# One array tile per head for the products with the states, another order of steps in each window, and x loaded first

## The chip, the cores and the metric

The kernel runs on one core of a Trainium2 chip. Its engines work side by side, each through its own list of instructions in order: TensorE (PE; its weight loads are shown as PEld), VectorE (DVE), ScalarE (ACT), GpSimd (POOL) and SyncE (SP), which here issues most transfers between HBM and the on-chip memory SBUF. TensorE writes into PSUM, eight banks of 128 x 512 float32. The metric is the device time of the whole program in microseconds (us).

## The reference

Three parts in a row, in float32 on the chip, with factors cut into a high and a low part where accuracy wants it:

```python
scores = scale * x @ state.T          # per head: 512 x 32
xread  = softmax(scores) @ state      # every x reads the 32 states
scores2 = scale * state @ x.T
sread  = softmax(scores2) @ x         # every state reads all x
t = concat([xread, sread])            # 4 batches x (512+32) tokens, 8 heads x 64 = 512 columns
h = t @ w_in;  g = where(h >= 1, h, where(h <= -1, 0, (h + 1)**2 / 4));  t = g @ w_out
h = t @ w_in2; g = max(h, 0) + log1p(exp(-abs(h)));                      t = g @ w_out2
```

The weights are 512 x 2048 and 2048 x 512 and arrive as 64-bit floats; 2,176 tokens go through.

## The kernel before, in words

The read of the states is not carried out for x: since `xread = a @ state`, the first layer for a batch is `a @ (state @ w_in)`, and the kernel makes G = state @ w_in for each batch, 256 columns of w_in (a *pair* of 128-column blocks, 8 pairs) at a time. These are the products with the states (`g_mm`, L404). A head has 64 of the 512 columns and 32 states, so one head's product is 64 rows deep and 32 columns wide on the array. Before, two heads share one product: `stb` holds both heads' states on the diagonal of a 128 x 64 block, with zeros beside them, and four products of 128 x 64 with 256 columns fill one PSUM bank. The scores (`scores`, L213) use the same blocks.

G is then cut in two by `g_split`: ScalarE copies it rounded (`gh`, L67), VectorE subtracts for the residue (`gl`, L70). Products of full accuracy are made of three, high x high, high x low and low x high; `ahi` and `alo` are the two parts of the softmax of the scores.

The main loop runs over 148 *windows*. A window is one 128-wide block of the hidden layer for one tile of tokens: 16 for each of batches 0, 1 and 2, 4 for the states that were read ("s"), 16 for batch 3, then five tiles of 16 for the second network. One pass of the loop works for three windows at once: `l1(w)` makes the first layer of the newest (six products, L501), `close(v)` ends the activation of the one before it on VectorE (L584), `l2(u)` adds the second layer of the window three back into four accumulators (L441 to L443). All engines take their instructions in the order in which the loop writes them. A pass of the loop gives: l1, then the products with the states on TensorE, then a first step of the attention of a coming batch (`hops`, one step per `yield`), `close`, `l2`, the split of second-layer weights (L67 `wh`, GpSimd `wl`), `act_open` (L573, L574), the rebuild of coming weights, `cut_hi`, `cut_lo`, then `g_split`, then the scaling of the next weights, then a second step of hops, and last the issue of a transfer.

Weights arrive as 64-bit numbers, a pair (1 MB) at a time, in one of two `ws` buffers. ScalarE scales the upper words in place (L107), VectorE shifts and ors the halves together (`rebuild`, L123 and L124; into `w1_p` for w_in, which traces show as `w`, and into `cv` for w_out). The plan is a list of due windows: `plan_pair(Pair(w1, True, p, W1), 2 * (p - 1))` and `plan_pair(Pair(w2, ...), 2 * p + 1)`; a pair is scaled in the pass before its due pass, and the transfer into a buffer is issued at the due pass of the pair two before it. The first w_in pair comes in `wh`, the second in `wl`, before the loop.

PSUM: two rotating banks "at" serve the products with the states, the scores, the transposes of x (L198) and of scores (`s_turn`) and the read by the states (L265); two "l1", four accumulators.

Of the kernel before, what the change touches and what calls it, by code (L numbers as in the profile page):

```python
# [18 lines left out]
def fused_kernel(ctx: ExitStack, tc: tile.TileContext, x, state, w1, w2, w3, w4, out):  # L19
# [43 lines left out]
    def bank(tag, bufs):  # L63
        return new(psum, [P, 512], F32, tag, bufs)

    def copy(dst, src):
# [80 lines left out]
    make_identity(nc, ident)  # L147
    stb = new(p1, [P, NJ, B, 2 * N], F32, "stb")
    nc.gpsimd.memset(stb, 0.0)
    x1s = new(p1, [P, NJ, B * N], F32, "x1s")  # L150
# [24 lines left out]
    def place_state(st):  # L175
        ps = bank("at", 2).rearrange("p (j c) -> p j c", j=NJ)
        for j in range(NJ):
            nc.tensor.transpose(ps[:, j, :], st[:, 2 * j : 2 * j + 2, :].rearrange("p e d -> p (e d)"), ident)
        for e in range(2):
            sl = slice(e * D, (e + 1) * D)  # L180
            nc.vector.tensor_copy(
                stb[sl, :, :, e * N : (e + 1) * N], ps[sl].rearrange("p j (b n) -> p j b n", n=N)
            )

# [4 lines left out]
    class Attn:  # L189
# [18 lines left out]

        def scores(self, g):
            self.ps[g] = bank("at", 2)  # L210
            for i in range(2):
                j = 2 * g + i
                nc.tensor.matmul(  # L213
                    self.ps[g][64 * i : 64 * i + 64, :], stb[:, j, self.b, :], self.xT[j], start=True, stop=True
                )

# [25 lines left out]
        def s_turn(self, g):  # L242
            self.ps[g] = bank("at", 2)
# [12 lines left out]

        def s_read(self, js):
            xb = xt[self.b]
            if 0 in js:
                self.ps["s"] = bank("at", 2)  # L260
            for j in js:
                for r in range(R):
                    for e in range(2):
                        c0 = (2 * (j % 2) + e) * N
                        nc.tensor.matmul(  # L265
                            self.ps["s"][e * D : (e + 1) * D, j * N : (j + 1) * N],
                            xb[:, r, 2 * j + e, :],
                            self.a2T[j // 2][:, r, c0 : c0 + N],
                            start=(r == 0),
                            stop=(r == R - 1),  # L270
                        )
# [35 lines left out]
        def hops(self):  # L307

            for js in ((0, 1), (2,), (3,)):
                ps = [bank("at", 2) for _ in js]  # L310
# [7 lines left out]
            self.scores(0)  # L318
            yield
            self.s_copy(0)  # L320
            yield
            self.scores(1)
            yield
            self.s_copy(1)
            self.blocks(0)
# [26 lines left out]
            yield  # L352
            self.s_read((0, 1))
            yield
            self.n_hi(0)
            if self.b < 3:
                self.n_lo(0)
            self.n_back(1)
            yield
            self.s_read((2, 3))  # L360
# [5 lines left out]
            self.s_out()  # L366
            yield
# [5 lines left out]
        def rest(self):  # L373
            yield
            for g in range(NG):
                self.s_max(g)
            yield
            yield
            for g in range(NG):
                self.s_exp(g)  # L380
            yield
            yield
            for g in range(NG):
                self.s_norm(g)
# [6 lines left out]
            self.s_read((0, 1, 2, 3))  # L391
            yield
            self.s_out()
            yield
# [11 lines left out]
    def g_split(b, p, ps):  # L406
        hi = new(p1, [P, NG * C2], F32R, "gh", 2)
        lo = new(p1, [P, NG * C2], F32R, "gl", 2)
        copy(hi, ps)
        sub(nc.vector, lo, ps, f32(hi))  # L410
        G[b, p] = [t.rearrange("p (g f) -> p g f", g=NG) for t in (hi, lo)]

# [118 lines left out]
    def evac(w):  # L531
        if w.ph == 1 and w.tl == "s":
# [3 lines left out]
            def pe():  # L536
                ps = bank("at", 2)
                for k in range(NK):
# [95 lines left out]
    def plan_g(i, b, p):  # L634
        def pe():
            ps = bank("at", 2)
            g_mm(b, p, ps)
            return lambda: g_split(b, p, ps)
# [39 lines left out]
    with tc.manual_schedule():  # L678
        nc.scalar.preload_act_table_set("natural_log_exp_and_others")
        st = load_state()  # L680
        early = [pair for a, pair in pairs[:4]]
# [7 lines left out]
        warm(8)  # L689
        first.scale()  # L690
        first.conv()
        ps = bank("l1", 2)
        g_mm(0, 0, ps)
        g_split(0, 0, ps)
        a0 = Attn(0)
# [4 lines left out]
        for j in range(NJ):  # L700
            a0.x_copy(j, ps[j], j % 2 == 0)
        for g in range(NG):
            a0.scores(g)
        for g in range(NG):
            a0.blocks(g, a0.ps[g])
            a0.n_sub(g, (nc.vector, nc.gpsimd)[g])
        for g in range(NG):
            a0.s_copy(g)
            a0.n_exp(g)
        early[0].scale()  # L710
# [74 lines left out]
```

## Time and profile before

| what | value |
|---|---|
| median of 3 runs | 771.84 us (771.06 to 772.34) |
| profiled execution, whole time | 772.06 us |
| its span, first to last instruction | 770.2 us |
| busy: PE, PEld | 743.0 (96%), 606.3 (79%) |
| busy: DVE, ACT, POOL | 437.3 (57%), 458.3 (60%), 103.7 (13%) |
| granted clock of TensorE, mean | 0.99 |
| HBM read, written | 42.47 MB, 8.91 MB |

Busy time is the time that an engine spent in instructions, whether or not anybody waited for them. Shares over the whole span mix stages: GpSimd's 13% are 6 or 7 tenths of the time near the start and nothing in the second half. Beside busy times the trace gives for each instruction what ended the wait before it, and from these the chain of work that ended last.

### The profile page before, as it was taken

The page shows a single profiled execution, that of the slowest core. Times are in us where ns is not written, and L with a number is a line of the kernel's source. Part 1 is how long each engine was busy: PE and PEld are TensorE (multiplying, and loading weights), DVE is VectorE, ACT ScalarE, POOL GpSimd, SP SyncE. Part 2 cuts the span into 40 slices and gives each one's busy share as a digit, 9 for nine tenths or more (in the row PEclk, how much of TensorE's full clock was granted, in tenths as well). Part 3 has the DMA queues.
Part 4 walks back from the last instruction along what each step waited for, and adds up shares of the span by engine and source line. Part 5 has one row for each costly group of instructions (what it writes and reads, how often), then busy time and mean ns, then how long its engine had stood idle before and what let it go on. Part 6 is the DMA issues. An engine that isn't in the chain of part 4 may idle for free.

```text
span 770.2 us, 9775 instructions
## 1 busy us (share of the span) xinstructions
PE 743.0 (96%) x3768; PEld 606.3 (79%) x3768; DVE 437.3 (57%) x695; ACT 458.3 (60%) x800; POOL 103.7 (13%) x60
## 2 busy tenths in 40 slices
PE   5599899999999999999999999999999999999997
PEld 4366677867767788777888888888889998998986
DVE  4877964245337424555599984554654554555543
ACT  3677675445545435566778775655655666566563
POOL 0265670002000001122222320000000000000000
PEclk9799999999999999999999999999999999999999
DMA  9466363300010003144343400300020002001001
GB/s 289 110 217 217 109 194 81 55 1 1 1 55 1 1 1 110 56 128 159 110 164 110 164 0 1 96 1 1 0 89 9 1 0 83 1 1 41 1 1 41
DMA packets 39582, 52.00 MB, mean 68 GB/s; under 512 B 19312, under 2 KB 21872, under 8 KB 39536
## 3 DMA queue, kind: packets, MB, share of 16 engines
q1 hardware_dynamic: 36912, 50.73, 21.1%
q10 hardware_dynamic: 2624, 0.66, 0.4%
q8 instruction: 29, 0.48, 0.3%
q14 instruction: 17, 0.14, 0.1%
HBM read 42.47 MB, written 8.91 MB: 67 GB/s over the span
## 4 chain that ended last, share of the span: by engine, by line
PE 92%; DVE 4%; ACT 2%; DMA 1%; POOL 1%; issue 0%; SPq 0%; DVEq 0%; ACTq 0%
PE acc L441 16%; PE acc L442 16%; PE acc L443 16%; PE l L501 10%; PE l L443 8%; PE l L441 8%; PE l L442 8%; PE at L404 4%; PE l L488 2%; PE at L265 1%; PE at L213 1%; DMA wh<-in_moe_w_in_dram 1%; DVE w L124 1%; PE at L198 1%; DVE w L123 1%; POOL wl L70 0%
## 5 line engine op out<-in xcount | busy, mean ns | idle before, releaser
L70 DVE TENSOR_TENSOR gtl<-tl,gth 128x384 fp32r<-128x384 f32 (+1 forms) x80 | 48.9, 611 | 148.6 <-ACT gth L67 148.6
L577 ACT ACTIVATE ta<-l 128x384 f32<-128x384 f32 (+1 forms) x80 | 42.8, 535 | 128.7 <-PE l L443 128.7
L573 ACT ACTIVATE ta<-l 128x512 f32<-128x512 f32 x68 | 40.6, 598 | 128.2 <-PE l L501 104.3
L70 DVE TENSOR_TENSOR gtl<-ta,gth 128x512 fp32r<-128x512 f32 x52 | 36.0, 692 | 136.6 <-ACT gth L67 136.6
L442 PE MATMUL acc<-wl,gth 128*128 128x512 f32 x288 | 113.3, 393 | 0.0
L441 PE MATMUL acc<-wh,gth 128*128 128x512 f32 x288 | 113.2, 393 | 0.0
L443 PE MATMUL acc<-wh,gtl 128*128 128x512 f32 x288 | 112.7, 391 | 0.0
L441 PE MATMUL acc<-gth,wh 128*128 128x512 f32 x256 | 104.7, 409 | 0.0
L443 PE MATMUL acc<-gth,wl 128*128 128x512 f32 x256 | 100.2, 391 | 0.4 <-POOL wl L70 0.4
L442 PE MATMUL acc<-gtl,wh 128*128 128x512 f32 x256 | 100.3, 392 | 0.0
L70 POOL TENSOR_TENSOR wl<-cv,wh 128x1024 fp32r<-128x1024 f32 x24 | 62.8, 2615 | 220.8 <-ACT wh L67 219.5
L443 PE MATMUL l<-x,wl 128*128 128x384 f32 (+1 forms) x192 | 68.7, 358 | 0.0
L441 PE MATMUL l<-x,wh 128*128 128x384 f32 (+1 forms) x192 | 68.6, 357 | 0.0
L442 PE MATMUL l<-x,wh 128*128 128x384 f32 (+1 forms) x192 | 68.5, 357 | 0.0
L443 PEld LDWEIGHTS acc<-wh,gtl 128*128 128x128 f32 x288 | 54.1, 188 | 12.2
L441 PEld LDWEIGHTS acc<-gth,wh 128*128 128x128 f32 x256 | 48.1, 188 | 19.1 <-issue 9.1
L441 PEld LDWEIGHTS acc<-wh,gth 128*128 128x128 f32 x288 | 54.1, 188 | 11.2 <-issue 0.8
L442 PEld LDWEIGHTS acc<-wl,gth 128*128 128x128 f32 x288 | 54.0, 188 | 10.0
L443 PEld LDWEIGHTS acc<-gth,wl 128*128 128x128 f32 x256 | 48.1, 188 | 11.6 <-POOL wl L70 0.8
L70 DVE TENSOR_TENSOR tl<-tl,ta 128x384 f32<-128x384 f32 (+1 forms) x80 | 55.3, 691 | 2.8
L588 DVE SCALAR_TENSOR_TENSOR ta<-tb,ta 128x384 f32<-128x384 f32 (+1 forms) x80 | 55.9, 698 | 0.0
L442 PEld LDWEIGHTS acc<-gtl,wh 128*128 128x128 f32 x256 | 48.2, 188 | 8.8
(114 smaller groups left out, 1376.2 us busy)
## 6 DMA issues: line engine op xcount, KB each, us to landing
ws<-in_moe_w_out_dram SPq DMA_DIRECT2D x16, 1024.0 KB, 4.8
ws<-in_moe_w_in_dram SPq DMA_DIRECT2D x14, 1024.0 KB, 5.5
xd<-xs SPq DMA_DIRECT2D x16, 256.0 KB, 2.9
out_dram<-xs SPq DMA_DIRECT2D x16, 256.0 KB, 2.5
x<-in_x_dram SPq DMA_DIRECT2D x14, 256.0 KB, 6.2
xs<-xd SPq DMA_DIRECT2D x8, 256.0 KB, 6.3
wh<-in_moe_w_in_dram SPq DMA_DIRECT2D x2, 512.0 KB, 5.5
wl<-in_moe_w_in_dram SPq DMA_DIRECT2D x2, 512.0 KB, 7.7
```

The source lines that it names most:

```text
L70: eng.tensor_tensor(dst, a, b, op=ALU.subtract)
L123: nc.vector.tensor_scalar(d, lo, 29, None, op0=ALU.logical_shift_right)
L124: nc.vector.scalar_tensor_tensor(d, hi, 3, d, op0=ALU.logical_shift_left, op1=ALU.bitwise_or)
L404: nc.tensor.matmul(o, stb[:, j, b, :], W1[p][:, j, :], start=True, stop=True)
L441: nc.tensor.matmul(o, lh, rh, start=first, stop=False)
L442: nc.tensor.matmul(o, lh, rl, start=False, stop=False)
L443: nc.tensor.matmul(o, ll, rh, start=False, stop=last)
L488: nc.tensor.matmul(w.h[:, i * P : (i + 1) * P], W1[f // 2][:, k, (f % 2) * P : (f % 2 + 1) * P], x1s[:, k, :], start=(k == 0), stop=(k == ...
L501: nc.tensor.matmul(w.h, l[:, g, f], r[:, g, :], start=i == 0, stop=i == len(terms) - 1)
L573: nc.scalar.activation(w.a, w.hc, AF.Relu, bias=1.0)
L577: nc.scalar.activation(w.a, w.hc, AF.Abs)
L588: nc.vector.scalar_tensor_tensor(w.a, w.b, 1.0, w.a, op0=ALU.subtract, op1=ALU.subtract)
```

## The change

Four things. The states lie in `stT` without zeros, and `heads` makes one product per head, 64 rows by 32 columns, on eight places of the array: the row half e, and the 32-column block j. The heads of the upper rows write one PSUM bank and those of the lower rows another. The rotating banks "at" become one tile `side` of two banks; steps that need one bank take its halves in turn (`at_bank`), products with the states and scores take both. The loop's pass puts the products with the states and `g_split` behind the scaling and the second step of hops. At the start, x is loaded ahead of all weights, its scores come before the first weights are rebuilt, and two multiplications and both residues go to GpSimd.

```diff
+    side = new(psum, [P, 2, 512], F32, "at")
+    def at_bank():
+        turn[0] ^= 1
+        return side[:, turn[0] ^ 1, :]
...
+    def heads(b, o, rhs):
+        for j in range(NJ):
+            for e in range(2):
+                rows = slice(e * D, (e + 1) * D)
+                nc.tensor.matmul(
+                    o(e)[j * N : (j + 1) * N, :], stT[rows, j, b * N : (b + 1) * N], rhs(j)[rows], start=True, stop=True
+                )
...
-    def g_mm(b, p, ps):
-        for j in range(NJ):
-            i = j % 2
-            o = ps.rearrange("p (g f) -> p g f", g=NG)[64 * i : 64 * i + 64, j // 2, :]
-            nc.tensor.matmul(o, stb[:, j, b, :], W1[p][:, j, :], start=True, stop=True)
+    def g_mm(b, p, two=None):
+        o = (lambda e: side[:, e, :C2]) if two is None else (lambda e: two[e][:, :C2])
+        heads(b, o, lambda j: W1[p][:, j, :])
...
-        plan_pair(Pair(w1, True, p, W1), 2 * (p - 1))
+        plan_pair(Pair(w1, True, p, W1), max(2 * p - 3, -1))
     for p in range(NP):
-        plan_pair(Pair(w2, False, p, W2, lambda: pools["b"]), 2 * p + 1)
+        plan_pair(Pair(w2, False, p, W2, lambda: pools["b"]), 2 * p)
...
-                plan_g(t0 + 2 * p - (1 if b == 0 else 2), b, p)
+                plan_g(t0 + 2 * p - 2, b, p)
...
         first = Pair(w1, True, 0, W1)
         first.load("wh", nc.sync)
-        load_x(0, [nc.scalar, nc.sync])
...
-            a0.n_norm(g, nc.vector)
+            a0.n_norm(g, (nc.vector, nc.gpsimd)[g])
+        for g in range(NG):
+            sub(nc.vector, lo[:, g, :], two[g][:, :C2], f32(hi[:, g, :]))
         for g in range(NG):
             a0.n_back(g)
             a0.n_hi(g)
-            a0.n_lo(g, nc.vector)
+            a0.n_lo(g, nc.gpsimd)
+        run(-1, "conv")
+        run(-1, "late")
...
-            rests = [f() for f in post] + run(i, "pe")
+            for f in post:
+                f()()
...
-            for f in rests:
-                f()
             run(i, "late")
             for g in list(gens.values()):
                 next(g, None)
+            run(i, "pe")
             run(i, "load")
```

(`load_x` now stands ahead of `first`.) In `hops` the two steps of scores become one, as do the two of the read by the states, and steps without work keep their places. In the changed kernel the small products have line 194, l1 508, l2 448 to 450, copies 75, residues 78, scaling 115, the rebuild 131 and 132, `close` 591 and `act_open` 580 and 581.

TensorE, the first three windows of the loop, before (`l1_46`, `l1_49` and `l1_58` are their first layers, `gh_21` and `gh_55` the first and second pair of G):

```order
L501 MATMUL l1_46_216<-ahi_23_139,gh_21_135 128x512 x2
L501 MATMUL l1_46_216<-alo_24_140,gh_21_135 128x512 x2
L501 MATMUL l1_46_216<-ahi_23_139,gl_22_136 128x512 x2
L501 MATMUL l1_49_232<-ahi_23_139,gh_21_135 128x512 x2
L501 MATMUL l1_49_232<-alo_24_140,gh_21_135 128x512 x2
L501 MATMUL l1_49_232<-ahi_23_139,gl_22_136 128x512 x2
L404 MATMUL at_50_239<-w1_1_48_226,stb_2_74 64x256 x4
L501 MATMUL l1_58_262<-ahi_23_139,gh_55_255 128x512 x2
L501 MATMUL l1_58_262<-alo_24_140,gh_55_255 128x512 x2
L501 MATMUL l1_58_262<-ahi_23_139,gl_56_256 128x512 x2
```

and now (`l1_46`, `l1_52` and `l1_60`):

```order
L508 MATMUL l1_46_229<-ahi_19_121,gh_32_176 128x512 x2
L508 MATMUL l1_46_229<-alo_20_122,gh_32_176 128x512 x2
L508 MATMUL l1_46_229<-ahi_19_121,gl_33_177 128x512 x2
L194 MATMUL at_1_69<-w1_1_44_218,stT_3_75 32x256 x8
L508 MATMUL l1_52_257<-ahi_19_121,gh_32_176 128x512 x2
L508 MATMUL l1_52_257<-alo_20_122,gh_32_176 128x512 x2
L508 MATMUL l1_52_257<-ahi_19_121,gl_33_177 128x512 x2
L508 MATMUL l1_60_282<-ahi_19_121,gh_49_251 128x512 x2
L508 MATMUL l1_60_282<-alo_20_122,gh_49_251 128x512 x2
L508 MATMUL l1_60_282<-ahi_19_121,gl_50_252 128x512 x2
```

The group for the second pair moved ahead of the first layer of window 1, and is eight small products in place of four.

ScalarE, window 3 before, up to the next window's first step (`gh_76` is a pair of G, `ws_65` weights that have just landed, `wh_84` a half of second-layer weights):

```order
L573 ACTIVATE ta_72_316<-l1_66_287 128x512
L574 ACTIVATE ta_72_316<-ta_72_316 128x512
L67 ACTIVATE gth_74_322<-ta_61_274 128x512
L67 ACTIVATE gh_76_326<-at_67_294 128x512
L107 ACTIVATE ws_65_285<-ws_65_285 128x1024
L67 ACTIVATE wh_84_365<-cv_73_319 128x1024
L573 ACTIVATE ta_86_369<-l1_81_335 128x512
```

and window 4 now, in which a copy of G stands again (`at_1` is the tile of two banks, `xT` the turned x of the next batch):

```order
L580 ACTIVATE ta_83_386<-l1_82_358 128x512
L581 ACTIVATE ta_83_386<-ta_83_386 128x512
L75 ACTIVATE gth_85_392<-ta_75_343 128x512
L115 ACTIVATE ws_79_354<-ws_79_354 128x1024
L75 ACTIVATE xT0_87_397<-at_1_69 128x512
L75 ACTIVATE xT1_88_399<-at_1_69 128x512
L75 ACTIVATE gh_89_409<-at_1_69 128x512
L75 ACTIVATE wh_93_439<-cv_84_389 128x1024
```

The scaling of `ws` and two copies of x now stand ahead of `gh`, which stood ahead of them.

VectorE at the end of the start, before (`alo_24` are the residues of the softmax, `ta_47` the activation of window 0, `w1_1` the second w_in pair, `cv_52` the first w_out pair):

```order
L298 STREAM_TRANSPOSE sa_44_207<-sa_37_180 128x512
L70 TENSOR_TENSOR alo_24_140<-sa_44_207,ahi_23_139 128x512
L123 TENSOR_SCALAR w1_1_48_226<-wl_13_99 128x512
L124 SCALAR_TENSOR_TENSOR w1_1_48_226<-wl_13_99,w1_1_48_226 128x512
L123 TENSOR_SCALAR w1_1_48_226<-wl_14_100 128x512
L124 SCALAR_TENSOR_TENSOR w1_1_48_226<-wl_14_100,w1_1_48_226 128x512
L584 SCALAR_TENSOR_TENSOR ta_47_223<-ta_47_223,l1_46_216 128x512
L123 TENSOR_SCALAR cv_52_248<-ws_15_103 128x1024
L124 SCALAR_TENSOR_TENSOR cv_52_248<-ws_15_103,cv_52_248 128x1024
L70 TENSOR_TENSOR gl_56_256<-at_50_239,gh_55_255 128x512
```

and now (`w1_1_44`, `cv_48` and `ta_47_236` are the same three):

```order
L307 STREAM_TRANSPOSE sa_43_214<-sa_36_183 128x512
L131 TENSOR_SCALAR w1_1_44_218<-wl_14_99 128x512
L132 SCALAR_TENSOR_TENSOR w1_1_44_218<-wl_14_99,w1_1_44_218 128x512
L131 TENSOR_SCALAR w1_1_44_218<-wl_15_100 128x512
L132 SCALAR_TENSOR_TENSOR w1_1_44_218<-wl_15_100,w1_1_44_218 128x512
L131 TENSOR_SCALAR cv_48_239<-ws_16_103 128x1024
L132 SCALAR_TENSOR_TENSOR cv_48_239<-ws_16_103,cv_48_239 128x1024
L78 TENSOR_TENSOR gl_50_252<-at_1_69,gh_49_251 128x512
L591 SCALAR_TENSOR_TENSOR ta_47_236<-ta_47_236,l1_46_229 128x512
```

The residue `alo` has left VectorE, and the first rebuild into `cv` and `gl` now stand ahead of the close of window 0.

## Rows read from the trace of the kernel before

**Rows 1.** Busy time by stage: the stretch (us), its length, busy us of each engine with its instructions in brackets, TensorE's granted clock, the share of time that the DMA engines were busy, GB/s. The cuts are the first step of window 0 on ScalarE (29.36), of window 16 (112.56), of window 68 (376.30), and the end.

```profile
0.00:29.36 29.36, 14.12 (x59) 10.25 (x60) 17.20 (x30) 9.13 (x14) 2.64 (x8) 0.79 0.84 223
29.36:112.56 83.20, 76.29 (x414) 55.91 (x415) 67.07 (x79) 61.15 (x94) 51.96 (x29) 0.99 0.52 174
112.56:376.30 263.74, 263.74 (x1475) 204.85 (x1474) 124.46 (x207) 140.62 (x245) 26.73 (x16) 1.00 0.19 55
376.30:770.20 393.90, 388.85 (x1824) 335.28 (x1822) 228.61 (x380) 247.41 (x448) 22.38 (x9) 1.00 0.13 42
```

**Rows 2.** The chain of work that ended last, over the whole span, as shares: by engine, and by engine, tile and line.

```profile
PE 92%; DVE 4%; ACT 2%; DMA 1%; POOL 1%; issue 0%; SPq 0%; DVEq 0%; ACTq 0%
PE acc L441 16%; PE acc L442 16%; PE acc L443 16%; PE l L501 10%; PE l L443 8%; PE l L441 8%; PE l L442 8%; PE at L404 4%; PE l L488 2%; PE at L265 1%; PE at L213 1%; DMA wh<-in_moe_w_in_dram 1%; DVE w L124 1%; PE at L198 1%; DVE w L123 1%; POOL wl L70 0%
```

**Rows 3.** The same chain in order of time, at small products and behind them: start (us), us, engine, tile, line, instructions.

```profile
60.40 1.01 PE at L404 x8
61.42 0.86 PE at L213 x4
62.28 0.43 PE acc L441
62.70 0.23 PE acc L442
...
65.22 1.40 PE l L501 x6
66.62 1.01 PE at L213 x4
...
103.07 0.90 PE at L265 x32
...
284.14 3.57 PE l L488 x32
```

**Rows 4.** TensorE's wait for the state over the span (us, how often, the longest), and the chain in the start, as in rows 3.

```profile
PE at L178 <- DMA xT<-in_state_dram: 3.9, 1, 3.9
...
15.98 0.73 DVE sa L224
24.80 0.69 DVE alo L70
```

**Rows 5.** Busy time in three stretches of the start, columns as in rows 1: with the weights under way, with x under way behind them, and with TensorE mostly idle.

```profile
12.00:18.00 6.00, 4.44 (x21) 2.96 (x20) 3.77 (x6) 1.68 (x3) 0.00 (x0) 0.86 1.04 397
19.50:23.50 4.00, 0.00 (x0) 0.00 (x0) 3.79 (x9) 1.73 (x3) 1.05 (x1) 0.63 1.32 220
20.51:30.75 10.24, 4.72 (x10) 3.39 (x11) 7.57 (x16) 4.34 (x8) 0.11 (x1) 0.50 0.41 67
```

**Rows 6.** The timeline of single instructions around one weight pair in the loading stage, by engine (ScalarE, VectorE, GpSimd, SyncE): start (us), us, engine, line, operation, out<-in, shapes, in square brackets the idle time before it and what ended it; and from the page the issues of w_in transfers: how many, KB each, us from issue to landing.

```profile
52.24 0.58 ACT L67 ACTIVATE gh<-at 128x512 fp32r<-128x512 f32 x1
52.72 1.14 ACT L107 ACTIVATE ws<-ws 128x1024 f32<-128x1024 f32 x1
54.23 1.05 ACT L67 ACTIVATE wh<-cv 128x1024 fp32r<-128x1024 f32 x1
44.54 0.68 DVE L123 TENSOR_SCALAR w<-ws 128x1024 uint32<-128x1024 uint32 x1
45.33 1.23 DVE L124 SCALAR_TENSOR_TENSOR w<-ws,w 128x1024 uint32<-128x1024 uint32 x1
47.27 2.10 DVE L123 TENSOR_SCALAR cv<-ws 128x1024 uint32<-128x1024 uint32 x1
49.48 2.12 DVE L124 SCALAR_TENSOR_TENSOR cv<-ws,cv 128x1024 uint32<-128x1024 uint32 x1
52.85 0.69 DVE L70 TENSOR_TENSOR gl<-at,gh 128x512 fp32r<-128x512 f32 x1 [1.25 <-ACT gh L67]
45.50 3.33 POOL L70 TENSOR_TENSOR wl<-cv,wh 128x1024 fp32r<-128x1024 f32 x1 [1.31 <-PE at L198]
46.59 0.37 SPq L95 DMA_DIRECT2D ws<-in_moe_w_in_dram  x1
ws<-in_moe_w_in_dram SPq DMA_DIRECT2D x14, 1024.0 KB, 5.5
```

**Rows 7.** From the loading stage, 26 to 116 us (the last row from 90 to 112): waits (the waiting instruction, what ended the wait, sum in us, count, the longest in us); the rebuilds of w_in, of w_out's residues and of others by tile (count, then shortest/median/longest ns, and the stretch); residues alo on GpSimd (count, busy us, mean ns, idle before).

```profile
ACT ws L107 <- DMA ws<-in_moe_w_in_dram: 2.5, 1, 2.5
PEld l L501 <- ACT gh L67: 3.8, 2, 1.9
PE at L404 <- DVE s L238: 1.4, 1, 1.4
L123 DVE TENSOR_SCALAR w<-ws x6: 684/686/2929, 35.1 to 90.9; 128x1024 uint32<-128x1024 uint32 x6
L124 DVE SCALAR_TENSOR_TENSOR w<-ws,w x6: 1224/1226/3248, 35.8 to 92.3; 128x1024 uint32<-128x1024 uint32 x6
L70 POOL TENSOR_TENSOR wl<-cv,wh x8: 2380/2905/3432, 35.9 to 111.6; 128x1024 fp32r<-128x1024 f32 x8
L70 POOL TENSOR_TENSOR alo<-sa,ahi 128x512 fp32r<-128x512 f32 x2 | 3.0, 1512 | 0.0
```

**Rows 8.** The timeline of ScalarE, columns as in rows 6: the first step of windows 2 and 12.

```profile
35.70 0.59 ACT L573 ACTIVATE ta<-l 128x512 f32<-128x512 f32 x1
91.34 0.60 ACT L573 ACTIVATE ta<-l 128x512 f32<-128x512 f32 x1
```

More of the change, by code (lines that the diff above doesn't have):

```diff
@@ L147, in fused_kernel @@
     make_identity(nc, ident)
-    stb = new(p1, [P, NJ, B, 2 * N], F32, "stb")
-    nc.gpsimd.memset(stb, 0.0)
+    stT = new(p1, [P, NJ, B * N], F32, "stT")
     x1s = new(p1, [P, NJ, B * N], F32, "x1s")
@@ L175, in place_state @@
     def place_state(st):
-        ps = bank("at", 2).rearrange("p (j c) -> p j c", j=NJ)
+        ps = at_bank().rearrange("p (j c) -> p j c", j=NJ)
         for j in range(NJ):
             nc.tensor.transpose(ps[:, j, :], st[:, 2 * j : 2 * j + 2, :].rearrange("p e d -> p (e d)"), ident)
[L179 to L183, printed above, removed]
+        nc.vector.tensor_copy(stT, ps)
+    def heads(b, o, rhs):
[5 more added lines that the diff above has]
+                )
     NB = S // N
@@ L207, in x_copy, with scores @@
                 nc.vector.tensor_copy(self.xT[j], ps)
[L209 to L215, printed above, removed]
+        def scores(self):
+            heads(self.b, lambda e: side[:, e, :], lambda j: self.xT[j])
+            self.ps.update((g, side[:, g, :]) for g in range(NG))
         def s_copy(self, g):
@@ L242, in s_turn @@
         def s_turn(self, g):
-            self.ps[g] = bank("at", 2)
+            self.ps[g] = at_bank()
             for r in range(R):
@@ L255, in s_keep, with s_read @@
             copy(t, self.ps[g])
-        def s_read(self, js):
+        def s_read(self):
             xb = xt[self.b]
-            if 0 in js:
-                self.ps["s"] = bank("at", 2)
-            for j in js:
+            self.ps["s"] = at_bank()
+            for j in range(NJ):
                 for r in range(R):
                     for e in range(2):
-                        c0 = (2 * (j % 2) + e) * N
+                        c0 = j * N
                         nc.tensor.matmul(
@@ L309, in hops @@
             for js in ((0, 1), (2,), (3,)):
-                ps = [bank("at", 2) for _ in js]
+                ps = [at_bank() for _ in js]
                 for j, t in zip(js, ps):
@@ L317, in hops @@
                 yield
-            self.scores(0)
+            self.scores()
             yield
             self.s_copy(0)
+            self.s_copy(1)
             yield
-            self.scores(1)
             yield
-            self.s_copy(1)
             self.blocks(0)
@@ L398, in fused_kernel, with g_tiles, g_split @@
     G = {}
-    def g_mm(b, p, ps):
-        for j in range(NJ):
-            i = j % 2
-            o = ps.rearrange("p (g f) -> p g f", g=NG)[64 * i : 64 * i + 64, j // 2, :]
-            nc.tensor.matmul(o, stb[:, j, b, :], W1[p][:, j, :], start=True, stop=True)
[L406 to L411, printed above, removed]
+    def g_mm(b, p, two=None):
+        o = (lambda e: side[:, e, :C2]) if two is None else (lambda e: two[e][:, :C2])
+        heads(b, o, lambda j: W1[p][:, j, :])
+    def g_tiles(b, p):
+        G[b, p] = [new(p1, [P, NG, C2], F32R, t, 2) for t in ("gh", "gl")]
+        return G[b, p]
+    def g_split(b, p):
+        hi, lo = g_tiles(b, p)
+        copy(hi, side[:, :, :C2])
+        sub(nc.vector, lo, side[:, :, :C2], f32(hi))
     class Win:
@@ L536, in pe @@
             def pe():
-                ps = bank("at", 2)
+                ps = at_bank()
                 for k in range(NK):
@@ L635, in pe @@
         def pe():
-            ps = bank("at", 2)
-            g_mm(b, p, ps)
-            return lambda: g_split(b, p, ps)
+            g_mm(b, p)
+            g_split(b, p)
         when(i, "pe", pe)
@@ L680, in fused_kernel @@
         st = load_state()
-        early = [pair for a, pair in pairs[:4]]
+        load_x(0, [nc.scalar, nc.sync])
+        early = [pair for a, pair in pairs[:3]]
         first = Pair(w1, True, 0, W1)
         first.load("wh", nc.sync)
-        load_x(0, [nc.scalar, nc.sync])
         early[0].load("wl", nc.sync)
@@ L701, in fused_kernel @@
             a0.x_copy(j, ps[j], j % 2 == 0)
-        for g in range(NG):
-            a0.scores(g)
+        a0.scores()
+        first.scale()
+        first.conv()
+        two = [bank("l1", 2) for _ in range(NG)]
+        g_mm(0, 0, two)
+        hi, lo = g_tiles(0, 0)
         for g in range(NG):
@@ L709, in fused_kernel @@
             a0.n_exp(g)
+        for g in range(NG):
+            copy(hi[:, g, :], two[g][:, :C2])
         early[0].scale()
         for g in range(NG):
-            a0.n_norm(g, nc.vector)
+            a0.n_norm(g, (nc.vector, nc.gpsimd)[g])
+        for g in range(NG):
+            sub(nc.vector, lo[:, g, :], two[g][:, :C2], f32(hi[:, g, :]))
         for g in range(NG):
```

15 lines of the change are left out of this document (5 added, 10 removed).

## The prediction

> **What bounds the kernel now.** I read the busy time by stage first [rows 1]. In the two late stages TensorE is busy for practically the whole stretch, 263.7 of 263.7 us between 112.6 and 376.3 and 388.9 of 393.9 behind that, at a granted clock of 1.00, while VectorE and ScalarE are half idle: there only TensorE's work counts. In the stretch from 29.4 to 112.6, windows 0 to 15, which I call the loading stage, TensorE idles 83.2 - 76.3 = 6.9 us and VectorE (67), ScalarE (61) and GpSimd (52 of 83 us) are all loaded, because the weights of the first two layers come in there. Before 29.4 TensorE is busy half the time. Then the chain of waits by line [rows 2]: 92% of it is TensorE, and of the lines that the change touches the products with the states have 4% (L404) and 1% (L213). At that point one would expect a gain. The third view is the order of time around one weight pair in the loading stage [rows 6], and it turned my forecast round.
>
> **The change part by part.** Durations come from the profiled execution, 772.06 us with a span of 770.2, so 1.86 lie outside the span; the median of the runs is 771.84. I sum against the span.
>
> *The eight small tiles.* A group of L404 (four heads' pairs) takes 1.01 us on the chain, and the first 128x512 product behind any small group takes 0.43 instead of 0.23, 0.20 for the change of tile [rows 3]. In the four full-width windows 32 records of 128 columns take 3.57 us, 0.112 each, so eight records of 256 columns at full width would take 1.79: the two column halves already run side by side. The new group is eight products of a quarter width and half height on eight different places of the array. Bounds: all eight side by side make two record slots instead of four, about 1.01 - 0.43 = 0.58 us, a gain of 0.43; if only the four columns run together and the two row halves follow each other, four slots again, a gain of 0; if the eight follow each other in pairs as now, 2.0 us, a loss of 1.0. I take 0.58, since the row that it is nearest to shows two tiles side by side with no loss. The Trainium skill (TensorE: Matmul & The Clock Gate, Part 3: Packing small matmuls) says that row and column tiles compose, with 16 tiles 10.6 times as fast as one after the other; by that the gain would be the same 0.43. Its page TensorEngine Tiling (Array Packing), under Restrictions and Gotchas, adds that different row tiles cannot write one PSUM bank at the same time; the change obeys by using two banks, and no run here shows what the other would cost.
> Behind window 15, where TensorE sets the pace, 24 of the 31 remaining groups stand: 24 x 0.43 = 10.3 us won. The scores were two groups in two windows, 0.86 and 1.01 and twice 0.20 [rows 3]; one group of eight takes about 0.9 + 0.2: 1.0 won in each of two batches behind window 15, and 0.2 in each for the second read of x (two groups of 0.90 become one, with one change of tile less): 2.4 won.
>
> *One buffer for all.* The two rotating banks become one pair of banks, `side`, and a group of products now needs both. Where the next window gives a small step to TensorE, that step stands behind only six products (1.40 us [rows 3]) while the banks come free after gh (0.58) and gl (0.69) and some 0.3 of hand-offs, 1.57. So such a step waits about 0.2, and pays 0.2 for a change of tile of its own where it shared one before; five steps per batch, two batches: 4 us. Late normalisations that held a step for 1.4 us at most before [rows 7] may add 1 to 3; I take 3.4 for these and the extra changes of tile. Late stages: -10.3 - 2.4 + 4 + 3.4 = -5.3 (from -12.7 if nothing waits, to 0).
>
> *The ring that the new order closes.* This is the main term. Before, ScalarE takes gh ahead of the scaling of the next weights: gh at 52.24, L107 at 52.72 [rows 6]. Now the order is L107 (line 115), then the copies of x, then gh, as the second order piece above shows. L107 waits for a transfer. That transfer (w_in, 5.5 us from issue to landing [rows 6]) is issued when VectorE has rebuilt the pair before the last one from the same buffer: w ended at 46.56, SyncE issued at 46.59 [rows 6]. And VectorE, which works in order, has gl and the window's L584 ahead of the next rebuild of w. So from one w transfer to the next, two windows later, the steps now stand in one line: 5.5 landing + 1.14 L107 + 0.58 gh + 0.69 gl + 0.69 L584 (of gl's size) + rebuild. Before, gh and gl were not in it, and L107 waited for w_in transfers 2.5 us in all, so there was a little slack but not much [rows 7].
> The rebuild: alone 0.69 + 1.23 = 1.9; the six in this stage reach 2.93 + 3.25 = 6.2 at worst; beside GpSimd's wl and gtl the cv pair took 2.10 + 2.12 = 4.2 [rows 6, 7]. In the old order the w rebuild began just ahead of wl (44.54 against 45.50) and mostly escaped. In the new one the wl of a state pair follows gh by one ScalarE copy (1.05), which is when w is rebuilt in odd windows, so each of them meets wl and gtl. I take 4.9, between the cv row and the worst: the ring is 13.5 us (10.5 to 14.8). The Trainium skill (SBUF — State Buffer, Who interferes with whom) calls the pair of ports between VectorE and GpSimd an exclusive lock, where the later one waits until the earlier instruction is over. The rows bear it out: L123 on cv began at 47.27 during wl and ended 0.5 us after it. By the lock a rebuild that begins just behind wl would take wl's 2.38 and gtl's 1.51 (as alo's) and its own 1.9, 5.8 (an estimate from rows), and the ring 14.4.
> Two windows took 55.6/5 = 11.1 us before, between the first ScalarE step of window 2 (35.70) and of window 12 (91.34) [rows 8]. Five rings lie there (even windows 2 to 10). In window 4 two copies of x (half of wh's size each, 1.06 together) and then the group itself with its tail (0.85) come between L107 and gh, since the group needs both banks: 15.4. In window 6 one copy: 14.95. Sum 3 x 13.5 + 15.4 + 14.95 = 70.9, against 55.6: +15.2 us. TensorE has nothing to fill these gaps with, so what it saves in this stage is lost. Bounds: with the rebuild at 1.9 the ring is 10.5 and the five make 55.9, +0; with 6.2 it is 14.8 and they make 77: +22. For windows 12 to 16, where the second read of x and the turned scores wait for gl, +1 (-1 to +3).
>
> *The start.* x is now first in the queues. 1 MB in 256-byte pieces at 220 GB/s takes 4.8 us behind the state (3.9 [rows 4]): x is there at 8.6 and the first weights 2.7 later, at 397 GB/s [rows 5]; rebuilt at 12.7, so VectorE's first block can follow at 12.7, not 15.98 [rows 4]. Two multiplications and residues go from VectorE to GpSimd (alo 0.69 [rows 4], L294 of the same size), but GpSimd needs 1.51 for an alo [rows 7] and two of them follow each other, beside rebuilds that fight with it. First window: 2.5 us earlier. But the rebuild of the next w (4 instructions, 2.2 us) and of the first cv (1.9), and gl, now stand ahead of the first L584 on VectorE (third order piece), and window 2 cannot write its bank before that: these 4.8 us eat the 2.5 up. I take 0 at window 2 (-2.5 to +2).
>
> Sum: 0 + 15.2 + 1 - 5.3 = +10.9, a span of 781.1 and a run of 783.0 us.
>
> **The rivals.**
> *The ring stays slack and TensorE's saving comes through.* Point of decision: whether the weights have landed when ScalarE comes to L107. For it: waits for w_in landings were only 2.5 us before, and TensorE is the bound by 92%. Against: gh and gl are put behind that landing, and five of six parts of the line are read from rows. Then: start -2.5, windows 0 to 15 seven groups -3.0, and the late stages without waits -12.7: 770.2 - 18.2 + 1.9 = 754, and 761 if the late waits of 7.4 come all the same. Chance 0.24, since the ring rests on how the rebuilds meet GpSimd's work, which no row of this order shows.
> *The ring is just as long as two windows were,* because the rebuilds escape wl: +0 in the loading stage, +1 behind it, and late stages at 0: 772 or so, within 0.2%, which is about what a measurement of this kernel can tell from no change. Chance 0.05.
> *Row halves do not run side by side.* The change then does not do what it says. For it: the profile shows two column halves together and no row halves [rows 3]. Then the 10.3 us of the late stages and 1.7 of the scores are not won: 783 + 12 = 795. Chance 0.08.
> *The clock falls in the gaps.* In the start TensorE idled and was granted 0.50, the lower level of 1.2 GHz, from 20.51 to 30.75; in the loading stage it kept 0.99 with gaps of up to 1.9 us [rows 1, 5, 7]. The ring of 15.4 against TensorE's 9 us of work leaves gaps of 5 to 6 us, as long as that in the start. If the lower level returns for one window each in 4 and 6, 4.2 us of products take 8.4, half of it inside the gap: +5, 788. Chance 0.10.
>
> **How the numbers follow.** The forecast itself has 0.53, its own range 773 (rebuilds half as contended) to 792. Slower by over 0.2%: 0.53 + 0.08 + 0.10 = 0.71; within: 0.05; faster: 0.24. The range 760 to 797 leaves out the half of the first rival in which nothing waits, 0.12, and the corner where the clock and the serial rows meet, 0.06. I forecast 783.
>
> **What would show it.** Right: ScalarE idle before the scaling of ws, released by the transfer, for more than 10 us in windows 2 to 11 (2.5 before); w_in transfers 13 to 16 us apart; TensorE idle before the small groups and released by a copy of x in windows 4 and 6; rebuilds of w of 2 us and more each; late groups of about 0.6 us. Wrong: TensorE idle under 8 us between windows 0 and 16 (the ring did not close), groups of 1 us or more (no eight tiles side by side), or a start that is over 3 us earlier at window 2.

## The result and the profile after

The changed kernel takes 781.33 us (median of 4 runs, 780.41 to 785.18) against 771.61 for the kernel before: 1.0137 times as long, 95% interval 1.0110 to 1.0164. The forecast was 783.0 with a range of 760 to 797. The profiled execution, the shortest of the four, took 780.41 us with a span of 778.6, so the span grew by 8.4. Times by stage and by window are read from the one profiled execution of each kernel.

The same stages as in [rows 1] first: the cuts are again the first ScalarE step of windows 0 and 16 and of the last window of the first network (number 67 counted from 0; rows 1 call it window 68, but it is this one that begins at 376.30).

```profile
core 0: us, PE busy (x) PEld busy (x) DVE busy (x) ACT busy (x) POOL busy (x), PEclk, DMA share, GB/s
0.00:27.53 27.53, 13.17 (x82) 8.21 (x90) 16.72 (x28) 9.81 (x16) 6.00 (x10) 0.82 0.87 238
27.53:129.75 102.22, 81.31 (x486) 58.44 (x487) 70.74 (x77) 60.91 (x94) 53.20 (x29) 0.86 0.48 155
129.75:384.76 255.01, 253.96 (x1675) 195.60 (x1674) 128.40 (x207) 143.06 (x245) 25.08 (x15) 1.00 0.16 52
384.76:778.60 393.84, 388.85 (x1824) 335.26 (x1822) 229.01 (x380) 247.47 (x448) 22.68 (x9) 1.00 0.13 42
```

The loading stage grew from 83.20 to 102.22 us while busy time grew by 5.0 us on TensorE, part of it at a lower clock, and by less than 4 on the others: the rest is waiting. TensorE idles 20.9 us there, against 6.9 before. The stage behind it shrank from 263.74 to 255.01, and the last one stayed. The loss and the gain stand in different stages, and the mean busy shares (PE 96% before, 95% after) hide both.

The chain of work that ended last, shares by engine, to be held against [rows 2]:

```profile
PE 85%; DMA 4%; ACT 4%; DVE 3%; POOL 2%; issue 2%; ACTq 0%; POOLq 0%; DVEq 0%
```

A bound of 92% TensorE became 85%; transfers, ScalarE and GpSimd entered the chain. The next three groups show the ring. First its timeline around one w_in transfer (columns as in [rows 6]; SyncE, ScalarE, VectorE, GpSimd, and SyncE again):

```profile
49.70 0.37 SPq L103 DMA_DIRECT2D ws<-in_moe_w_in_dram  x1
...
55.03 1.10 ACT L115 ACTIVATE ws<-ws 128x1024 f32<-128x1024 f32 x1 [4.13 <-DMA ws<-in_moe_w_in_dram]
56.04 1.06 ACT L75 ACTIVATE xT<-at 128x512 f32<-128x512 f32 x2
58.37 0.60 ACT L75 ACTIVATE gh<-at 128x512 fp32r<-128x512 f32 x1 [1.26 <-PE at L194]
...
59.00 0.69 DVE L78 TENSOR_TENSOR gl<-at,gh 128x512 fp32r<-128x512 f32 x1 [6.82 <-ACT gh L75]
59.60 0.68 DVE L591 SCALAR_TENSOR_TENSOR ta<-ta,l 128x512 f32<-128x512 f32 x1
60.20 2.71 DVE L131 TENSOR_SCALAR w<-ws 128x1024 uint32<-128x1024 uint32 x1
62.95 1.23 DVE L132 SCALAR_TENSOR_TENSOR w<-ws,w 128x1024 uint32<-128x1024 uint32 x1
...
59.99 2.38 POOL L78 TENSOR_TENSOR wl<-cv,wh 128x1024 fp32r<-128x1024 f32 x1 [6.70 <-ACT wh L75]
...
64.25 0.37 SPq L103 DMA_DIRECT2D ws<-in_moe_w_in_dram  x1
```

Read it as a circle: issue at 49.70, landing at about 55, scaling, copies of x, the group, gh, gl, close, rebuild, and the next issue at 64.25, as soon as the rebuild has freed the buffer. VectorE and GpSimd both stand idle for 6.7 to 6.8 us and are then started by ScalarE at nearly the same moment, 59.0 and 60.0; that is why the rebuild meets `wl` every time. The issues of w_in stand at 36.55, 49.70, 64.25, 79.12 and 92.36: rings of 13.15, 14.55, 14.87 and 13.24 us.

The waits that belong to it between 26 and 132 us (sum, count, longest), and the rebuild of w in the same stretch (count, shortest/median/longest ns):

```profile
ACT ws L115 <- DMA ws<-in_moe_w_in_dram: 14.0, 5, 4.1
PE at L194 <- ACT xT L75: 9.0, 2, 7.0
L131 DVE TENSOR_SCALAR w<-ws x6: 2707/2721/2755, 31.5 to 101.6; 128x1024 uint32<-128x1024 uint32 x6
L132 DVE SCALAR_TENSOR_TENSOR w<-ws,w x6: 1227/2192/2343, 34.3 to 104.4; 128x1024 uint32<-128x1024 uint32 x6
```

In [rows 7] the wait for w_in was 2.5 us in all, and the median rebuild 0.69 + 1.23. Now it is 2.72 + 2.19. Not one of the six shifts escapes, and of the second halves only the one in the timeline above does (1.23).

Last, a small group in the late stage, in the chain in order of time, against [rows 3]:

```profile
141.85 0.59 PE at L194 x16
142.45 1.58 PE l L508 x6
```

A group takes 0.59 in place of 1.01; the six products behind it take 1.58 in place of the 1.40 that they take with no group ahead of them, for the change of tile. (A product has two records here, as before.)

### The profile page after: what moved, and what is told of

It reads as the page before. It is cut to its first block, busy times and chain, and to the rows that moved or that the text cites. A ratio compares the mean times of both kernels' runs of the same rounds, so it can differ in the third digit from the quotient of the medians.

```text
span 778.6 us, 10313 instructions
## 1 busy us (share of the span) xinstructions
PE 737.3 (95%) x4056; PEld 597.5 (77%) x4056; DVE 444.9 (57%) x692; ACT 461.3 (59%) x801; POOL 107.0 (14%) x62
## 4 chain that ended last, share of the span: by engine, by line
PE 85%; DMA 4%; ACT 4%; DVE 3%; POOL 2%; issue 2%; ACTq 0%; POOLq 0%; DVEq 0%
PE acc L448 15%; PE acc L449 15%; PE acc L450 15%; PE l L508 10%; PE l L450 8%; PE l L448 8%; PE l L449 8%; DMA ws<-in_moe_w_in_dram 3%; PE at L194 2%; PE l L495 2%; PE at L274 1%; DMA x<-in_x_dram 1%; POOL wl L78 1%; POOL gtl L78 1%; ACT ta L580 1%
## 5 line engine op out<-in xcount | busy, mean ns | idle before, releaser
L78 POOL TENSOR_TENSOR wl<-cv,wh 128x1024 fp32r<-128x1024 f32 x24 | 58.8, 2452 | 234.4 <-ACT wh L75 234.4
L78 DVE TENSOR_TENSOR gtl<-ta,gth 128x512 fp32r<-128x512 f32 x52 | 38.5, 741 | 90.7 <-ACT gth L75 90.7
L78 DVE TENSOR_TENSOR gl<-at,gh 128x512 fp32r<-128x512 f32 x31 | 21.3, 687 | 67.9 <-ACT gh L75 67.8
L508 PE MATMUL l<-ahi,gh 128*128 128x512 f32 x128 | 45.5, 437 | 12.3 <-ACT ahi L75 8.2
```

The source lines that it names most:

```text
L78: eng.tensor_tensor(dst, a, b, op=ALU.subtract)
L508: nc.tensor.matmul(w.h, l[:, g, f], r[:, g, :], start=i == 0, stop=i == len(terms) - 1)
```

## The experiments

"Windows 2 to 12" below is the time between the first ScalarE steps of these two windows: 55.64 us before, 73.05 in the changed kernel.

**The scaling behind gh.** In the changed kernel only the order of three steps in a pass is altered:

```diff
-            run(i, "late")
             for g in list(gens.values()):
                 next(g, None)
             run(i, "pe")
+            run(i, "late")
```

> The changed kernel, with the scaling of the next weights put behind gh in each pass (hops' second step, products with the states and their split, then the scaling). Ring theory: gh no longer stands behind a landing, so the line landing, scaling, gh, gl, close, rebuild is cut; windows 2 to 12 take 56 to 60 us in place of 73.05 and the kernel takes about 766 us (762 to 771), under the kernel before. Rival, the shared buffer: the group still needs both banks and still stands behind the copies of x, so most of the 17 us stays: 776 or more. Rival, the clock: the gaps and with them the low clock go only if the ring does, so this run alone does not part the two.

It took 765.22 us, 0.9924 (0.9907 to 0.9940) of the kernel before: faster than both. Windows 2 to 12 took 54.08. The group still needs both banks and still stands behind the copies of x; the rival of the shared buffer is out as the main cause. Its waits between 26 and 116 us:

```profile
ACT ws L115 <- DMA ws<-in_moe_w_out_dram: 0.8, 1, 0.8
```

No wait of the scaling for a w_in transfer is left, where the changed kernel had 14.0 us. But the rebuild has changed as well:

```profile
L131 DVE TENSOR_SCALAR w<-ws x6: 686/686/2897, 31.3 to 85.3; 128x1024 uint32<-128x1024 uint32 x6
L132 DVE SCALAR_TENSOR_TENSOR w<-ws,w x6: 1225/1226/2135, 32.1 to 88.3; 128x1024 uint32<-128x1024 uint32 x6
```

In this order it begins ahead of `wl`, and five of the six escape. So the run takes gh out of the line and shortens the rebuild at once; how the 19.0 us won in windows 2 to 12 divide between the two it doesn't tell. The run with wl on VectorE, below, parts them.

**Only the copies of x ahead of the scaling.**

```diff
-            run(i, "late")
             for g in list(gens.values()):
                 next(g, None)
+            run(i, "late")
             run(i, "pe")
```

> The changed kernel, with hops' second step (the copies of x) put ahead of the scaling, gh still behind it. Ring theory: the rings without copies stay at 13.2 us and those with copies (14.6 and 14.9) fall to 13.2, so about 3 us are won: 778 us (775 to 780). Rival, the shared buffer: once the copies do not wait for a landing, both banks are free early and most of the loss goes: 768 or less.

777.82 us (777.33 to 780.85), 3.5 under the changed kernel. The issues of w_in stand at 36.73, 49.98, 63.37, 76.54 and 89.92: every ring is now 13.2 to 13.4, and the two of 14.6 and 14.9 are gone. TensorE no longer waits long for the copies, yet the loss is still there:

```profile
ACT ws L115 <- DMA ws<-in_moe_w_in_dram: 15.7, 5, 4.2
PE at L194 <- ACT xT L75: 1.8, 1, 1.8
```

So gh behind the landing is what keeps the loss, and the copies are the smaller part of it.

**gh behind the scaling, in the kernel before.** Nothing else of the change is in it:

```diff
-            for f in rests:
-                f()
             run(i, "late")
+            for f in rests:
+                f()
```

> The kernel before, with gh and gl alone put behind the scaling (old tiles, old buffers, old start). Ring theory: the same ring closes, 13.5 us with a rebuild of 4.9 beside GpSimd's work, so windows 2 to 12 grow from 55.6 to 65 to 71 us and the kernel takes 781 to 787 us; if the rebuilds escape GpSimd here, the ring is 10.5 and the kernel takes 772 to 775. Rival, the shared buffer or the small tiles as the cause: neither is in this kernel, so 772.

784.83 us (782.49 to 786.67), 1.0175 (1.0154 to 1.0196) of the kernel before. This one line makes a loss larger than the whole change does. Windows 2 to 12 took 63.84, a little under the 65 expected; the issues are 12.4 us apart (38.67, 51.13, 63.53, 75.96), since here a rebuild of the first four takes 4.0 us instead of 4.9: in two of them the shift alone is stretched, in the other two the shift-and-or alone.

```profile
L123 DVE TENSOR_SCALAR w<-ws x6: 689/1994/2941, 34.6 to 101.5; 128x1024 uint32<-128x1024 uint32 x6
L124 DVE SCALAR_TENSOR_TENSOR w<-ws,w x6: 1225/2737/3311, 37.4 to 102.8; 128x1024 uint32<-128x1024 uint32 x6
```

Windows 12 to 16 took 1.5 us more than before, and window 2 began 0.8 later, which makes up the rest of its span of 780.7 (the profiled execution is the shortest of the four).

**wl on VectorE.** The changed kernel with the second part of the ring cut instead of the first: the residue of the second-layer weights, 2.4 us on GpSimd, goes to VectorE behind the rebuild.

```diff
-            sub(nc.gpsimd, lo, self.v, f32(hi))
+            if self.w is w2:
+                behind.append(lambda: sub(nc.vector, lo, self.v, f32(hi)))
+            else:
+                sub(nc.gpsimd, lo, self.v, f32(hi))
...
             run(i, "conv")
+            for f in behind:
+                f()
+            behind.clear()
```

> The changed kernel, with the residue wl of the second-layer weights of the first network taken from GpSimd to VectorE and put behind the rebuild of the same pass. Ring theory with contention: the w rebuild falls from 4.9 to 1.9 us (up to 3 if it still meets gtl on GpSimd), the ring from 13.2 to 10.2 to 11.4, and the kernel takes 766 to 773 us. Without contention as a cause (the rebuild is slow for another reason): the rebuild stays at 4.9 and the time at 781, or above it for the work added to VectorE.

768.11 us (766.52 to 768.96). Windows 2 to 12 took 59.83. The rebuild, in count and shortest/median/longest ns:

```profile
L133 DVE TENSOR_SCALAR w<-ws x6: 682/688/703, 33.2 to 90.4; 128x1024 uint32<-128x1024 uint32 x6
L134 DVE SCALAR_TENSOR_TENSOR w<-ws,w x6: 1225/1226/1226, 33.9 to 91.2; 128x1024 uint32<-128x1024 uint32 x6
```

Not one of the six is stretched any more, though VectorE has more work. The order of the steps is that of the changed kernel; taking 3 us out of each ring gives back 13.2 of the 17.4 us. GpSimd's `wl` beside the rebuild is thus shown as the cause of the 4.9 us, and this stretching makes three quarters of the loss in windows 2 to 12. The scaling still waits for w_in, though less than the 14.0 us above:

```profile
ACT ws L117 <- DMA ws<-in_moe_w_in_dram: 4.3, 3, 2.0
```

So putting gh behind the landing closes the ring, and it costs as much as it does because what gh sets off on GpSimd then meets the rebuild in each ring.

**TensorE's gap filled.** Products that nobody reads keep TensorE busy until the group comes:

```diff
+            for _ in range({4: 30, 6: 8}.get(i, 0)):
+                nc.tensor.matmul(v.h[:, :P], ident, ident, start=True, stop=True)
             run(i, "pe")
```

> The changed kernel, with 30 products of 128 columns that nobody reads put into TensorE's gap ahead of the products with the states in window 4, and 8 in window 6 (they write the bank of the window before, which is closed by then). Nothing of the ring is changed; the work behind the two gaps, which ran at half the clock (l1 2.87 and 2.68 us in place of 1.58, the groups 1.11 and 0.67 in place of 0.59), should run at the full one. Clock as a cost of its own: about 1.8 us less in window 4 and 1.3 in window 6, 778 us (777 to 780). Ring alone: the time behind each landing is hidden by the next landing, 781; above 782 if the filling outlasts the gaps.

781.77 us (780.93 to 782.99): no change beside 781.33, as expected if the ring alone sets the time. Busy time behind the gap of window 4, the changed kernel first (columns as in [rows 1]):

```profile
57.16:61.20 4.04, 4.04 (x24) 2.54 (x25) 2.20 (x3) 1.54 (x2) 1.21 (x1) 0.50 0.01 2
```

and with the filling:

```profile
57.22:60.30 3.08, 3.08 (x29) 2.11 (x29) 1.68 (x3) 2.25 (x4) 0.69 (x1) 1.00 0.01 5
```

After 7.0 us of idling the granted clock was 0.50, the level of 1.2 GHz; with the gap filled it was 1.00, and window 5 began 1.7 us earlier (59.56 against 61.22). Still the next w_in transfer was issued at 64.89, later than the 64.25 above: GpSimd's `gtl` could begin earlier too, at 61.98 instead of 63.09, and so came ahead of the second half of the rebuild:

```profile
62.62 2.19 DVE L132 SCALAR_TENSOR_TENSOR w<-ws,w 128x1024 uint32<-128x1024 uint32 x1
```

2.19 in place of 1.23. What the clock gave back in this window, the contention took. The filling of window 6 ended 2.9 us before its group and the clock fell again, so there, and in window 11, this run doesn't test the price of the clock.

**The start of before in the changed kernel.** x behind the first weights, G of the first pair ahead of the scores, and (in part):

```diff
-            a0.n_norm(g, (nc.vector, nc.gpsimd)[g])
+            a0.n_norm(g, nc.vector)
...
-            a0.n_lo(g, nc.gpsimd)
+            a0.n_lo(g, nc.vector)
```

> The changed kernel with the start of the kernel before: first weights ahead of x, G of the first pair ahead of the scores, normalisation and residues alo on VectorE. My term for the start: window 0 begins 2 us later (29.4) and window 2 within 2 us of the changed kernel's 35.4, so 782 us (780 to 784). Rival: the new start is worth what it wins at window 0 or more, 784 and above; or it is a loss by its residues on GpSimd, under 780.

782.31 us (781.74 to 784.18). Window 0 began at 28.78 (27.53 in the changed kernel), window 2 at 36.89 (35.43). The new start is worth about 1 us by the medians, which is no more than the spread of either kernel's runs.

**Both cuts.** The scaling behind gh, and wl on VectorE.

> Both cuts at once: the scaling behind gh, and the residue wl on VectorE behind the rebuild. Ring theory: with the scaling last the line through the landing is slack already, so the second cut adds little: 763 us (761 to 766). Rival, contention as a cost of its own beside the ring: another 3 us or more, under 761; VectorE overloaded in its place: above 766.

761.39 us (758.50 to 763.34), 0.9873 (0.9849 to 0.9897) of the kernel before; the best of all. The second cut is worth 3.8 us on top of the first, more than the 2 I expected of it; the time lies at the edge between my range (761 to 766) and the rival's (under 761). Little of this is the rebuild's, since with the scaling last only one of the six was still stretched. There it was `wl` that came second and took 3.3 to 3.5 us in five of six cases, in place of 2.4, and `gtl` stands behind it on GpSimd. What goes is the wait of ScalarE's first step of a window for `gtl` (the first cut alone, then both cuts):

```profile
ACT ta L580 <- POOL gtl L78: 9.2, 5, 2.3
ACT ta L585 <- POOL gtl L78: 0.2, 1, 0.2
```

So GpSimd's part of the contention also costs where the ring is slack. That the 3.8 us lie in this wait is read from the traces; no run takes it away alone. In the profiled execution, at 758.50 the shortest of the four, windows 2 to 12 took 49.26 us, and TensorE is busy for 73.0 of the 80.0 us of the loading stage, at nearly the full clock; this stage and the one behind it:

```profile
27.78:107.82 80.04, 72.97 (x486) 53.47 (x487) 65.06 (x85) 60.78 (x94) 30.89 (x21) 0.98 0.64 198
107.82:362.85 255.03, 253.98 (x1675) 195.59 (x1674) 128.40 (x207) 142.92 (x245) 25.08 (x15) 1.00 0.17 52
```

**The scaling behind gh, with the start of before.**

> The scaling behind gh, with the start of the kernel before. In the run with the scaling last window 2 began at 37.3, later than in the kernel before (35.7), since rebuilds met the residues alo on GpSimd. My term for the start: the two starts are worth the same within 2 us at window 2: 765 us (763 to 767). Rival, the new start as a loss: under 763; as a gain: above 767.

766.58 us (765.65 to 767.89), 1.4 above the run with the new start and within the 763 to 767 expected. By the medians of the two comparisons the new start wins 1.0 to 1.4 us; neither difference is clear of the noise.

**The old products in the best kernel.** Two heads per product, with zeros beside them, all else as in the kernel of both cuts (the layout of the states and the second read of x follow; not shown):

```diff
-        for j in range(NJ):
-            for e in range(2):
-                rows = slice(e * D, (e + 1) * D)
-                nc.tensor.matmul(
-                    o(e)[j * N : (j + 1) * N, :], stT[rows, j, b * N : (b + 1) * N], rhs(j)[rows], start=True, stop=True
-                )
+        for j in range(NJ):
+            i = j % 2
+            nc.tensor.matmul(o(j // 2)[64 * i : 64 * i + 64, :], stb[:, j, b, :], rhs(j), start=True, stop=True)
```

> The kernel of both cuts (scaling last, wl on VectorE; 761.4 us) with the old products: four of 128 rows by 64 columns per group, two heads with zeros beside them, in the same two banks, and all else as it is. My term for the small tiles: 0.42 us per group (1.01 against 0.59), 24 groups behind window 15 and 0.4 to 0.9 for each of two scores: the stretch behind window 16 grows by 11 to 12 us and the kernel takes 772 to 775 us. Rival, the small tiles give back what they win by changes of tile and waits: 762 to 766, and the late stages won for another reason.

774.68 us (773.35 to 776.42), 13.3 above. Windows 16 to 67 took 271.04 us (113.20 to 384.24, where the second network takes its first step) instead of 260.53 (107.82 to 368.35): the small tiles are worth 10.5 us there, a little under the 11 to 12 expected; the rest of the 13.3 lies in the loading stage. A group and what follows it, in the chain:

```profile
125.73 1.01 PE at L203 x8
126.75 1.60 PE l L515 x6
```

The group is back at 1.01, while the products behind it take the same 1.58 to 1.60: the change of tile costs as much behind four products as behind eight.

**The row halves one after the other.** The two loops of `heads` change places, in the changed kernel.

> The changed kernel with the eight products of a group written upper row half first and then the lower half, in place of turn by turn. If all eight run side by side wherever they stand in the order, a group still takes 0.59 us in the late stages and the kernel 781. If only neighbours in the order overlap, so that the halves need to alternate, a group takes about 1.0 and the kernel 790 or more.

781.21 us (two runs), and the group still takes 0.59:

```profile
133.50 0.59 PE at L194 x16
```

## Why the prediction was right

By its own terms, in us of the span, from the first ScalarE steps of windows:

| term | forecast | measured |
|---|---|---|
| start, to window 2 | 0 | 35.43 - 35.70 = -0.3 |
| ring, windows 2 to 12 | +15.2 | 73.05 - 55.64 = +17.4 |
| windows 12 to 16 | +1 | 21.27 - 21.22 = 0 |
| late stages | -5.3 | (255.01 - 263.74) + (393.84 - 393.90) = -8.8 |
| sum | +10.9 | +8.4 |

The terms erred in both directions: the ring was taken 2.2 us too small, the late stages 3.5 and windows 12 to 16 about 1 too large. That the sum came within 2.5 us is in part luck. The two terms for windows 2 to 16 are also good to 1 or 2 us only: the run with the row halves apart, which has the same order of steps, has 72.05 and 22.75 where the table has 73.05 and 21.27.

*The ring* is the mechanism that was named. The rebuild taken at 4.9 us measured 2.72 + 2.19 = 4.9; the plain ring of 13.5 measured 13.15 and 13.24, the one with two copies of x 14.55 for 15.4, the one with one copy 14.87 for 14.95 (its parts add up to 14.88). The signs that were asked for are there: 14.0 us of waits of the scaling for w_in, four issues in a row 13 to 15 us apart (the next, 19.2 us on, is at the end of the stage, where the kernel before has 17.4), TensorE released by a copy of x in windows 4 and 6, rebuilds of 2 us and more each, late groups of 0.59 us. The runs cut it at two places (gh ahead of the scaling, wl off GpSimd), and either cut gives most of the time back; and closed it in the kernel before with one line. What the term lacked lies in windows 10 to 12: the first four rings took 55.8 us for the 57.4 forecast, and the rest up to window 12 took 17.2 for 13.5. There two exponentials also stand between the scaling and gh, and the transposes of the scores wait 4.3 us for gl. I had counted that ring as one without copies. A third part may be the low clock (see the rivals).

*The small tiles* gave 0.42 us per group, forecast as 0.43. The forecast counts 24 groups behind window 15; they are 23, since one stands in window 14, and 23 x 0.42 = 9.7 us. All eight run side by side, in whichever order they are written.

*The late waits* were mis-sized. The step "so such a step waits about 0.2, and pays 0.2 for a change of tile of its own", with its 4 and 3.4 us, made 7.4. The last experiment but one measures it: with the old products, the new order and the one buffer take 271.04 us from window 16 to the second network, against 381.80 - 112.56 = 269.24 before. Together with what the merged scores save, that is +1.8, not +5 or more; TensorE idles 255.01 - 253.96 = 1.05 us in this stage in all. The term was a count of places where a step could wait, each priced as if it did.

*The start* came out as forecast at window 2 and was 1.8 us early at window 0 for the forecast 2.5. One multiplication went to GpSimd and not two, as the diff shows. Undone, the start costs 1.0 to 1.4 us by the medians, within its bounds.

*The rivals.* That the ring stays slack asked for no waits at the landing: there were 14.0 us, and TensorE idled 20.9 us in the loading stage, where under 8 would have shown the forecast wrong. That the row halves would follow each other asked for groups of about 1.0: they took 0.59. The low clock came, 0.50 behind a gap of 7.0 us. Its price of 5 us was too high by its own working: 4.2 more in each of two windows, half of it in the gap, is 4.2 in all. In window 4 its removal bought nothing, since `gtl` came earlier and stretched the rebuild. In window 6 the run with the start of before and the one with the halves apart were granted 1.00 (from 71 to 76 us; 0.66 in the changed kernel), and their rings there were 14.69 and 14.71 us for 14.87: the low clock cost no more than 0.2 us in it. In window 11 it stands on the chain of the changed kernel, where products of the second layer take 0.43 us in place of 0.23:

```profile
101.19 1.11 PE at L255 x4
102.30 0.43 PE acc L448
```

Nine of them in a row do so, 1.8 us. With the halves apart the clock was higher there (0.69 from 101.0 to 106.5 us, against 0.52), and windows 10 to 12 took 16.34 us in place of 17.23; yet windows 12 to 16 took 1.5 us more, and the time of the kernel was the same. What the clock costs in window 11 stays open.

## What to carry to other kernels

An engine that takes its work in order turns a wait into a wait for all that stands behind it: before moving a step behind an instruction that waits for a transfer, follow what the step releases, and look whether it leads back to the issue of that transfer. If it does, the sum of the circle is the period, however idle the engines look; and it can be cut at more than one of its parts, here by moving one line. Look also at what each step of the circle sets off elsewhere: most of this loss came from a GpSimd subtraction that the new order started just ahead of the rebuild. A gain on the engine that bounds the late stages and a loss in the loading stage add up in the total, so both have to be summed stage by stage.

## What was not expected of the hardware

- Starting an engine earlier can cost time: `gtl` on GpSimd, begun 1.1 us earlier, stretched a VectorE shift-and-or from 1.23 to 2.19 us.
- In these traces VectorE and GpSimd took turns, whole instructions at a time. In the timeline above the shift began at 60.20, 0.2 us behind `wl`, and ended 0.5 us after it (62.91 against 62.37); in six of six cases it took 2.71 to 2.76 instead of 0.69, while `wl` kept its 2.37 to 2.42. Then the shift-and-or went first in its turn, 1.23, and `gtl`, begun at 63.09 behind it, took 2.24 instead of 1.29. That is what the Trainium skill (SBUF — State Buffer, Who interferes with whom) calls an exclusive lock, and the traces agree. By it the forecast had 5.8 us for a rebuild behind both `wl` and `gtl`; measured were 4.9. `wl` had a start of 0.2 us, `gtl` takes 1.29 alone and not the 1.51 of an `alo`, and it went ahead of the second half in five of six cases; where it didn't, the rebuild took 4.0.
- The order in which eight products on eight places of the array are written made no difference: 0.59 us either way.
